# Sums of second-layer weights on GpSimd in 16 tasks, another place for a table of token weights, and another order of one chunk

## The chip, the cores and the metric

The kernel runs on one core of one Trainium2 chip. The metric is the device time of one execution in microseconds (us). The core has five engines that run their own instruction streams in order and wait for each other by semaphores: PE (TensorE, the matmuls), DVE (VectorE), ACT (ScalarE), POOL (GpSimd), and SP, which here issues nearly all DMA transfers. A transfer that waits on SP holds up every transfer behind it on SP.

## The reference

Block-sparse attention over 4 batches of 768 tokens (8 heads of 64), then a mixture of 4 experts on its 3072 x 512 result, weighted by the normalised `domain_probs`:

```python
p = domain_probs / (domain_probs.sum(-1, keepdims=True) + 1e-09)
for e in range(E):
    h = np.maximum(x @ w1[e], 0.0)
    out += p[:, e:e + 1] * (h @ w2[e])
```

Here `x` is 3072 x 512, `w1[e]` 512 x 1024, `w2[e]` 1024 x 512, everything in fp32.

## The kernel before

**Work and stages.** Attention of batch 0 comes first. After that the expert stage of batch b runs interleaved with the attention of batch b + 1. The hidden width of all experts is cut into 8 chunks of 512 (`NCH`). Each fp32 operand of a product is kept as two parts, a rounded one and the rest, and a product of two operands takes three matmuls. ACT writes the rounded part (a cast), POOL or DVE the rest (a subtraction).

**Fewer products.** The chunk products are split into 2 x 2 blocks and done in seven block products instead of eight, which needs sums and differences of blocks of the weights. Chunk 0 of each batch is "plain": eight block pairs, 16 products, in the order of the table `FIRST` (L455). An item (s, half, g) of it is one result, made by two products (k = 0 and 1); s and half name a quarter of the chunk's hidden width, g a half of the tokens. The other chunks follow `ORDER` (L450), with 7 products for each s.

**Weights, once made, are kept.** In batch 0, `operands()` (L494) turns raw first-layer weights `r1` into tiles `wo` (L513 on ACT, L514 on POOL), of which `NWO` = 7 exist, and stores each in DRAM (`kept1`, L492). Later batches load them back in the order of use (L528). Each `next(weights)` makes or loads one more tile; it can go only into a tile whose products are done. `split_w2` (L559) does the same for the second layer as batch 0 uses it (L550 ACT, L551 POOL, store L561).

**Sums of the second layer.** Later batches also need block sums of `w2`. `sums_w2()` (L572) makes them during batch 0, as a generator that is advanced by one `yield` for each step of the expert stage. It has 32 tasks of 8 steps: load 2 x 128 KB (L587), four 128 x 128 subtractions on DVE (L598, L599, L601, L602), a cast of 128 x 512 on ACT (L606), the rest on POOL (L608), four stores of 128 KB (L614). Rows in these transfers are 512 bytes long. Four tiles `r3` rotate.

**Batch 0 on PE.** `first` (L644) makes hidden values in PSUM; ACT (`hh`, L651) and DVE (`hl`, L652) turn each into two parts; DVE also combines block products (`p` L677, `u` L684 and L686, `z` L689). `second` (L695) multiplies with `w2` (L703) into three PSUM tiles `po`, which DVE adds up as `oacc` (L716 for chunk 0, L718). PE can start the next use of a `po` tile only when `oacc` has read it.

**From batch 0 to batch 1.** After the last step of `first`, `experts()` drains what is left of `sums_w2`, closes the pool `raw` (which holds `r1`, `r2`, `r3`), and opens in its memory a pool for `pb`, the token weights spread over partitions; two of them are loaded (L729). From batch 1 on, `first7` (L734) multiplies each hidden block with `pb` (L745, DVE), which releases its PSUM tile, and `second7` (L849) makes the second layer from `ho` and `w2o`, with `w2o` loaded by `again2` (L543). The results of batch 0 go out from `oacc` at L720.

**What sets the order.** Every engine's order is the program's (`manual_schedule`), so the generators' steps fix it:

```python
if c == 0:
    half, k, g = n
    i = [item for item, _ in FIRST].index((s, half, g))
    if k == 0:
        W[0] = ps_m.tile([P, HS], F32, name="vw"[i % 2], bufs=2 - i % 2)
    product(W[0], w, x, k == 0)
    if k == 1:
        finish(half, g, W.pop(0))
        for _ in range(FIRST[i][1]):
            next(weights, None)
```

A weight tile of the plain chunk is used twice, first for g = 0 and last for g = 1, and is free after that.

## Time and profile before

| | |
|---|---|
| time, three executions | 1297.15 us median (1295.63, 1297.15, 1300.03) |
| profiled execution | 1300.79 us, of which the span from first to last instruction is 1298.7 us |
| busy over the span: PE, DVE, ACT, POOL | 1228.8, 901.1, 526.9, 789.0 us |
| granted TensorE clock, mean | 0.984 |
| DMA | 336.25 MB, mean 259 GB/s |

The profile is one execution. A row of the timeline gives the start in us, the duration in us, engine, line, operation and tiles, and in brackets how long the engine sat idle before it and what ended that. A row of the windows gives a stretch's busy us of PE, PEld (weight loading), DVE, ACT and POOL, the granted clock as a share of full speed, the busy share of the DMA engines, and GB/s. Times in all views count from the first instruction. The attention of batch 0 ends at about 104 us, batch 0's experts run to 443 us, batch 1's plain chunk starts there.

### The profile page before, as it was taken

The page shows a single profiled execution, that of the slowest core. Times are in us where ns is not written, and L with a number is a line of the kernel's source. Part 1 is how long each engine was busy: PE and PEld are TensorE (multiplying, and loading weights), DVE is VectorE, ACT ScalarE, POOL GpSimd, SP SyncE. Part 2 cuts the span into 40 slices and gives each one's busy share as a digit, 9 for nine tenths or more (in the row PEclk, how much of TensorE's full clock was granted, in tenths as well). Part 3 has the DMA queues.
Part 4 walks back from the last instruction along what each step waited for, and adds up shares of the span by engine and source line. Part 5 has one row for each costly group of instructions (what it writes and reads, how often), then busy time and mean ns, then how long its engine had stood idle before and what let it go on. Part 6 is the DMA issues. An engine that isn't in the chain of part 4 may idle for free.

```text
span 1298.7 us, 33124 instructions
## 1 busy us (share of the span) xinstructions
PE 1228.8 (95%) x12575; PEld 1121.0 (86%) x12575; DVE 901.1 (69%) x1898; ACT 526.9 (41%) x1261; POOL 789.0 (61%) x702
## 2 busy tenths in 40 slices
PE   6778999999999989999999999999999999999997
PEld 3557778787788778999999989999999999999997
DVE  5455678878787546777766666767776776666667
ACT  3564446554554224444442324444443323222221
POOL 5443547766765255667664665767664777666663
PEclk9889999999999989999999999999999999999999
DMA  8667689999999967889877976989897768888774
GB/s 250 160 197 274 200 279 312 327 318 330 340 329 299 322 203 218 273 266 276 267 247 214 309 224 208 280 260 280 272 258 220 239 221 273 254 261 256 241 242 154
DMA packets 258793, 336.25 MB, mean 259 GB/s; under 512 B 20715, under 2 KB 169804, under 8 KB 258636
## 3 DMA queue, kind: packets, MB, share of 16 engines
q1 hardware_dynamic: 251552, 311.08, 75.7%
q0 software_dynamic: 7040, 23.07, 6.1%
q8 instruction: 99, 1.62, 0.5%
q14 instruction: 58, 0.48, 0.1%
q10 hardware_dynamic: 44, 0.00, 0.0%
HBM read 266.39 MB, written 67.68 MB: 257 GB/s over the span
## 4 chain that ended last, share of the span: by engine, by line
PE 62%; DVE 5%; DMA 3%; issue 1%; SPq 1%; ACT 0%; POOL 0%; DVEq 0%; POOLq 0%; ACTq 0%
PE w L633 16%; PE u L867 15%; PE v L633 12%; PE v L867 11%; PE o L293 2%; PE po L703 2%; PE tp L280 2%; DMA wo<-kept 1%; PE s L258 1%; PE s L253 1%; PE sw L327 1%; DVE ha L745 1%; DVE xo L404 1%; DVE tot L877 1%; PE ow L358 1%
## 5 line engine op out<-in xcount | busy, mean ns | idle before, releaser
L791 POOL TENSOR_TENSOR ho<-ha,ho 128x768 fp32r<-128x768 f32 x165 | 322.1, 1963 | 240.4 <-ACT ho L790 239.8
L633 PE MATMUL w<-xo,wo 128*128 128x384 f32 x1536 | 317.9, 343 | 16.6 <-DMA wo<-kept 6.4
L633 PEld LDWEIGHTS w<-xo,wo 128*128 128x128 f32 x1536 | 272.3, 189 | 30.8 <-DMA wo<-kept 6.1
L790 ACT CAST ho<-ha 128x768 fp32r<-128x768 f32 x168 | 139.4, 836 | 276.7 <-DVE ha L745 92.4
L633 PE MATMUL v<-xo,wo 128*128 128x384 f32 x1200 | 246.0, 341 | 2.7 <-DVE hl L652 2.2
L867 PE MATMUL u<-ho,w2o 128*128 128x384 f32 x1128 | 232.2, 341 | 0.3 <-issue 0.3
L633 PEld LDWEIGHTS v<-xo,wo 128*128 128x128 f32 x1200 | 214.6, 190 | 8.8 <-DVE hl L652 2.8
L867 PEld LDWEIGHTS u<-ho,w2o 128*128 128x128 f32 x1128 | 200.5, 189 | 2.5 <-issue 1.2
L867 PE MATMUL v<-ho,w2o 128*128 128x384 f32 x888 | 182.1, 341 | 1.9 <-issue 1.5
L867 PEld LDWEIGHTS v<-ho,w2o 128*128 128x128 f32 x888 | 156.8, 188 | 3.7 <-issue 2.0
L877 DVE TENSOR_TENSOR tot<-v,tot 128x384 f32<-128x384 f32 x184 | 97.7, 550 | 58.8 <-PE v L867 56.5
L877 DVE TENSOR_TENSOR tot<-u,tot 128x384 f32<-128x384 f32 x180 | 98.9, 552 | 55.3 <-PE u L867 52.6
L703 PE MATMUL po<-w2o,hh 128*128 128x512 f32 x384 | 124.8, 406 | 9.9 <-DVE oacc L718 6.6
L271 ACT ACTIVATE p<-p,mx 128x256 f32<-128x256 f32 (+1 forms) x192 | 95.4, 498 | 82.1 <-DVE mx L268 82.1
L745 DVE SCALAR_TENSOR_TENSOR ha<-ha,pb 128x384 f32<-128x384 f32 x126 | 123.4, 979 | 4.4
L138 POOL DMA_INDIRECT v<-in_vr_dram,vidx x88 | 85.3, 969 | 67.4 <-PE o L293 21.2
L514 POOL TENSOR_TENSOR wo<-r,wo 128x256 fp32r<-128x256 f32 x92 | 75.3, 823 | 74.5 <-ACT wo L513 57.2
L268 DVE CUSTOM_DVE_ANT_1 p<-s,mask 128x256 f32<-128x256 f32 (+1 forms) x192 | 69.7, 417 | 32.1 <-PE s L258 32.0
L703 PEld LDWEIGHTS po<-w2o,hh 128*128 128x128 f32 x384 | 68.3, 188 | 21.6 <-DVE oacc L718 9.8
L703 PE MATMUL po<-w2o,hl 128*128 128x512 f32 x192 | 75.7, 394 | 0.0
L293 PEld LDWEIGHTS o<-v,pt 128*32 128x32 f32 x2816 | 48.6, 116 | 17.7 <-issue 12.8
L293 PE MATMUL o<-v,pt 128*32 128x64 f32 x2816 | 57.4, 229 | 6.8 <-issue 3.5
(149 smaller groups left out, 1659.7 us busy)
## 6 DMA issues: line engine op xcount, KB each, us to landing
w2o<-kept SPq DMA_DIRECT2D x336, 256.0 KB
wo<-kept SPq DMA_DIRECT2D x318, 256.0 KB
kept<-wo SPq DMA_DIRECT2D x106, 256.0 KB
v<-in_vr_dram SPq DMA_DIRECT2D x44, 384.0 KB
kept<-w2o SPq DMA_DIRECT2D x32, 512.0 KB
r<-in_w_dram SPq DMA_DIRECT2D x16, 512.0 KB
r<-in_w_dram SPq DMA_DIRECT2D x32, 256.0 KB
r<-in_w_dram SPq DMA_DIRECT2D x64, 128.0 KB
```

The source lines that it names most:

```text
L138: nc.gpsimd.indirect_dma_start(out=v[:, i, 1], out_offset=None, in_=vr, element_offset=b * S * DM, in_offset=bass.IndirectOffsetOnAxis(ap= ...
L268: nc.vector.tensor_tensor_reduce(p.rearrange("p (a b) -> p a b", b=BLOCK), s[h][:n, i], mk, -SCALE, 3.0e38, ALU.add, ALU.min, mx[:n])
L271: nc.scalar.activation(p, p, AF.Exp, bias=mx[:n], scale=-1.0, accum_out=self.sums[:n, m:m + 1])
L293: nc.tensor.matmul(o[cs, m], self.pt[:, 2 * m + k, cs], vs[c][:, k, e], start=k == 0, stop=k == 1)
L514: nc.gpsimd.tensor_sub(o[:, 1], src, f32(o[:, 0]))
L633: nc.tensor.matmul(ps, w[:, wi, t], x[:, xi, t], start=fresh and m == 0, stop=m == 3 * KH - 1, skip_group_check=not fresh)
L703: nc.tensor.matmul(p, a[:, js], w[:, i], start=f == 0 and n == 0, stop=f == FT - 1 and n == 2)
L745: nc.vector.scalar_tensor_tensor(block(g, half), src, 0.0, q, op0=ALU.max, op1=ALU.mult)
L790: nc.scalar.copy(o[:, 0], src)
L791: eng.tensor_sub(o[:, 1], src, f32(o[:, 0]))
L867: nc.tensor.matmul(ps, w[:, j, wi, ds], h[:, hi, j], start=fresh and m == 0, stop=m == 5, skip_group_check=not fresh)
L877: nc.vector.tensor_add(t, ps, t)
```

## The change

1. `sums_w2` has 16 tasks of 16 steps. A task takes both halves of a pair of rows: one load of 512 KB, four 128 x 256 subtractions on POOL instead of DVE in steps 0 to 3, the two casts (ACT) and rests (POOL) of 128 x 512 in steps 5 and 7, and four stores of 256 KB in steps 8 and 10. Rows in these transfers are 2 KB long. Two tiles `r3` of twice the size rotate. Bytes and the number of steps are the same.
2. `r1` gets a pool of its own, `raw1`, opened before `raw`. The pool of `pb` therefore lies over the two `r1` tiles. Draining `sums_w2`, closing and loading `pb` come three steps of `first` earlier.
3. In later batches the plain chunk follows `FIRST7`: the items (1, 0, 1) and (1, 1, 0) change places, and one weight is loaded after each product with g = 1, where two were loaded after each second one. Batch 0 keeps `FIRST`.

```diff
@@ -49,6 +49,7 @@
     xp = ctx.enter_context(tc.tile_pool(name="xp", bufs=1))
     wp = ctx.enter_context(tc.tile_pool(name="wp", bufs=4, side="right"))
     only_raw = ctx.enter_context(ExitStack())
+    raw1 = only_raw.enter_context(tc.tile_pool(name="raw1", bufs=2, side="right"))
     raw = only_raw.enter_context(tc.tile_pool(name="raw", bufs=2, side="right"))
     dram = ctx.enter_context(tc.tile_pool(name="dram", bufs=1, space=bass.MemoryType.DRAM))
     at = ctx.enter_context(tc.tile_pool(name="at", bufs=2))
@@ -454,6 +455,7 @@
 
     FIRST = [((0, 0, 0), 0), ((0, 1, 0), 0), ((1, 0, 0), 0), ((0, 0, 1), 2), ((0, 1, 1), 2),
              ((1, 1, 0), 0), ((1, 0, 1), 2), ((1, 1, 1), 2)]
+    FIRST7 = [(0, 0, 0), (0, 1, 0), (1, 0, 0), (0, 0, 1), (0, 1, 1), (1, 0, 1), (1, 1, 0), (1, 1, 1)]
     XOF = {(0, 0): 1, (1, 0): 2, (0, 1): 7, (1, 1): 3}
     PLAIN8 = [(s, (i, k)) for s in range(2) for i in range(2) for k in range(2)]
 
@@ -476,7 +478,7 @@
 
     def load_w1(c, s):
         if c < NCH:
-            r1[c, s] = raw.tile([P, 2, 2, KH, P], F32, name="r1")
+            r1[c, s] = raw1.tile([P, 2, 2, KH, P], F32, name="r1")
             nc.sync.dma_start(r1[c, s], w1[c, s])
 
     def load_w2(n):
@@ -571,49 +573,46 @@
 
     def sums_w2():
 
-
-        cols = P
-        tasks = [(c, j, h) for c in range(NCH) for j in range(2) for h in range(2)]
+        half = DM // 2
+        tasks = [(c, j) for c in range(NCH) for j in range(2)]
         r3 = {}
-
-        def part(t, s, h):
-            return t.rearrange("p (d e) -> p d e", d=2)[:, :, h * cols:(h + 1) * cols]
 
         def load(i):
             if i < len(tasks):
-                c, j, h = tasks[i]
-                r3[i] = raw.tile([P, 2, 2, cols], F32, name="r3", bufs=4)
-                for s in range(2):
-                    nc.sync.dma_start(r3[i][:, s], part(w2[c, 2 * s + j], s, h))
+                c, j = tasks[i]
+                r3[i] = raw.tile([P, 2, DM], F32, name="r3", bufs=2)
+                nc.sync.dma_start(r3[i], w2[c, j::2].rearrange("s p e -> p s e"))
 
         load(0)
-        load(1)
         for _ in range(8):
             yield
-        for i, (c, j, h) in enumerate(tasks):
-            load(i + 2)
-            yield
+        for i, (c, j) in enumerate(tasks):
             r = r3.pop(i)
-            b11, b12, b21, b22 = (r[:, s, d] for s in range(2) for d in range(2))
-            nc.vector.tensor_sub(b11, b12, b11)
-            nc.vector.tensor_sub(b12, b22, b12)
-            yield
-            nc.vector.tensor_sub(b22, b22, b11)
-            nc.vector.tensor_sub(b21, b21, b22)
-            yield
-            yield
-            hi = later["t"].tile([P, 2, 2, cols], F32R, name="t2", bufs=2)
-            nc.scalar.copy(hi, r)
-            lo = r.bitcast(F32R)
-            nc.gpsimd.tensor_sub(lo, r, f32(hi))
-            yield
-            yield
-            for s in range(2):
-                k = kept2[c, 1, s, j] if h else keep2(c, 1, s, j)
-                for m, t in enumerate((f32(hi), r)):
-                    nc.sync.dma_start(part(k[:, m], s, h), t[:, s])
-            yield
-            yield
+            b11, b12, b21, b22 = (r[:, s, d * half:(d + 1) * half] for s in range(2) for d in range(2))
+            sums = (b11, b12, b11), (b12, b22, b12), (b22, b22, b11), (b21, b21, b22)
+            parts = {}
+
+            def part(s):
+                hi = later["t"].tile([P, DM], F32R, name="t2", bufs=2)
+                nc.scalar.copy(hi, r[:, s])
+                nc.gpsimd.tensor_sub(r[:, s].bitcast(F32R), r[:, s], f32(hi))
+                parts[s] = f32(hi), r[:, s]
+
+            def store(s):
+                k = keep2(c, 1, s, j)
+                for m, t in enumerate(parts[s]):
+                    nc.sync.dma_start(k[:, m], t)
+
+            for step in range(16):
+                if step < 4:
+                    nc.gpsimd.tensor_sub(*sums[step])
+                if step == 2:
+                    load(i + 1)
+                if step in (5, 7):
+                    part((step - 5) // 2)
+                if step in (8, 10):
+                    store((step - 8) // 2)
+                yield
 
     spare = sums_w2()
 
@@ -746,14 +745,14 @@
 
         if c == 0:
             half, k, g = n
-            i = [item for item, _ in FIRST].index((s, half, g))
+            i = FIRST7.index((s, half, g))
             if k == 0:
                 W[0] = ps_m.tile([P, HS], F32, name="vw"[i % 2], bufs=2 - i % 2)
             product(W[0], w, x, k == 0)
             if k == 1:
                 finish(half, g, W.pop(0))
-                for _ in range(FIRST[i][1]):
-                    next(weights, None)
+            if g:
+                next(weights, None)
             return
         if n in (5, 2, 3):
             v = ps_m.tile([P, HS], F32, name="v", bufs=2)
@@ -917,7 +916,7 @@
                 after_first = True
                 if p > L + 2:
                     next(spare, None)
-                if p == len(one):
+                if p == len(one) - 3:
                     for _ in spare:
                         pass
                     only_raw.close()
@@ -935,7 +934,7 @@
         for b in range(1, B):
             for c in range(NCH):
                 one += ([(b, c, s, n) for s, n in ORDER] if c else
-                        [(b, 0, s, (half, k, g)) for (s, half, g), _ in FIRST for k in range(2)])
+                        [(b, 0, s, (half, k, g)) for s, half, g in FIRST7 for k in range(2)])
                 ends.append(len(one))
                 two += [(b, c, i) for i in range(len(SEQ))]
                 due += [len(one) + 2 + i for i in range(len(SEQ))]
```

How the instructions stand on the engines, at the three places.

**A task of sums, late in batch 0.** DVE before; `r` is the tile `r3`, `hl` the rest of a hidden block, `p` a combined block product, `po` the PSUM tile of the second layer:

```order
L689 TENSOR_TENSOR z_6790<-w,z_6790 128x384
L652 SCALAR_TENSOR_TENSOR hl_6903<-z_6790,hh_6902 128x384
L601 TENSOR_TENSOR r_6631<-r_6631 128x128
L602 TENSOR_TENSOR r_6631<-r_6631 128x128
L652 SCALAR_TENSOR_TENSOR hl_6934<-w,hh_6933 128x384
L598 TENSOR_TENSOR r_6761<-r_6761 128x128
L599 TENSOR_TENSOR r_6761<-r_6761 128x128
L677 TENSOR_TENSOR p_6956<-w,p_6956 128x384
L652 SCALAR_TENSOR_TENSOR hl_7003<-p_6956,hh_7002 128x384
L601 TENSOR_TENSOR r_6761<-r_6761 128x128
L602 TENSOR_TENSOR r_6761<-r_6761 128x128
L718 SCALAR_TENSOR_TENSOR oacc<-po,pr,oacc 128x512 x3
```

DVE now, at the same place:

```order
L688 TENSOR_TENSOR z_6618<-w,z_6618 128x384
L651 SCALAR_TENSOR_TENSOR hl_6728<-z_6618,hh_6727 128x384
L651 SCALAR_TENSOR_TENSOR hl_6757<-w,hh_6756 128x384
L676 TENSOR_TENSOR p_6775<-w,p_6775 128x384
L651 SCALAR_TENSOR_TENSOR hl_6822<-p_6775,hh_6821 128x384
L717 SCALAR_TENSOR_TENSOR oacc<-po,pr,oacc 128x512 x3
```

The sums are gone from between the block products and `oacc`. POOL now, for one task (L608 are the sums, L598 the rests; L516 and L553 are what L514 and L551 were):

```order
L608 TENSOR_TENSOR r_5597<-r_5597 128x256
L516 TENSOR_TENSOR wo<-r_5277,wo 128x256
L608 TENSOR_TENSOR r_5597<-r_5597 128x256 x3
L516 TENSOR_TENSOR wo<-r_5277,wo 128x256
L598 TENSOR_TENSOR r_5597<-r_5597,t_5916 128x512
L516 TENSOR_TENSOR wo<-r_5590,wo 128x256
L598 TENSOR_TENSOR r_5597<-r_5597,t_5936 128x512
```

The four sums now stand in the queue in which POOL also makes the first-layer weights.

**The end of batch 0 on SP.** Before; `kept_0_1_10` is the seventh of the eight weights of batch 1's plain chunk:

```order
L528 DMA wo<-kept_0_0_11_2395 128x512
L528 DMA wo<-kept_0_1_00_2425 128x512
L528 DMA wo<-kept_0_1_01_2583 128x512
L614 DMA kept_7_1_0_1_7041<-t_7090 128x2x128
L614 DMA kept_7_1_0_1_7041<-r_6887 128x2x128
L614 DMA kept_7_1_1_1_7044<-t_7090 128x2x128
L614 DMA kept_7_1_1_1_7044<-r_6887 128x2x128
L528 DMA wo<-kept_0_1_10_2590 128x512
L729 DMA pb<-prt 128x6x128 x2
L720 DMA out_dram<-oacc 128x512 x3
L561 DMA kept_7_0_1_1_7039<-w2o 128x1024
```

Now:

```order
L530 DMA wo<-kept_0_0_11_2398 128x512
L604 DMA kept_7_1_0_1_6877<-t_6848 128x512
L604 DMA kept_7_1_0_1_6877<-r_6629 128x512
L604 DMA kept_7_1_1_1_6880<-t_6864 128x512
L604 DMA kept_7_1_1_1_6880<-r_6629 128x512
L728 DMA pb<-prt 128x6x128 x2
L530 DMA wo<-kept_0_1_00_2428 128x512
L530 DMA wo<-kept_0_1_01_2586 128x512
L530 DMA wo<-kept_0_1_10_2593 128x512
L719 DMA out_dram<-oacc 128x512 x3
```

The last stores of the sums and the two loads of `pb` stand ahead of three weight loads that they stood behind.

**Batch 1's plain chunk on PE, last ten products.** Before; `xo1`, `xo2` belong to g = 0, `xo7`, `xo3` to g = 1, and a `wo` number is a tile of weights:

```order
L633 MATMUL w_7298<-xo7_7170,wo_6962 128x384 x6
L633 MATMUL w_7298<-xo3_7185,wo_7006 128x384 x6
L633 MATMUL v_7317<-xo7_7170,wo_7030 128x384 x6
L633 MATMUL v_7317<-xo3_7185,wo_7059 128x384 x6
L633 MATMUL w_7335<-xo1_7148,wo_7126 128x384 x6
L633 MATMUL w_7335<-xo2_7139,wo_7313 128x384 x6
L633 MATMUL v_7354<-xo7_7170,wo_7079 128x384 x6
L633 MATMUL v_7354<-xo3_7185,wo_7104 128x384 x6
L633 MATMUL w_7373<-xo7_7170,wo_7126 128x384 x6
L633 MATMUL w_7373<-xo3_7185,wo_7313 128x384 x6
```

Now:

```order
L632 MATMUL w_7110<-xo7_6982,wo_6781 128x384 x6
L632 MATMUL w_7110<-xo3_6997,wo_6825 128x384 x6
L632 MATMUL v_7129<-xo7_6982,wo_6846 128x384 x6
L632 MATMUL v_7129<-xo3_6997,wo_6875 128x384 x6
L632 MATMUL w_7147<-xo7_6982,wo_6908 128x384 x6
L632 MATMUL w_7147<-xo3_6997,wo_6928 128x384 x6
L632 MATMUL v_7171<-xo1_6960,wo_6946 128x384 x6
L632 MATMUL v_7171<-xo2_6951,wo_7117 128x384 x6
L632 MATMUL w_7185<-xo7_6982,wo_6946 128x384 x6
L632 MATMUL w_7185<-xo3_6997,wo_7117 128x384 x6
```

The eighth weight (`wo_7313` before, `wo_7117` now) is loaded into the tile that the first of these products frees. It was used as the sixth of these products, and is now used as the eighth.

## The prediction

> **What bounds the kernel now.** I read the page first.
>
> ```profile
> PE 1228.8 (95%) x12575; PEld 1121.0 (86%) x12575; DVE 901.1 (69%) x1898; ACT 526.9 (41%) x1261; POOL 789.0 (61%) x702
> ```
>
> PE is the bound, and the matmuls do not change. Only time in which PE is idle, or runs at a lower clock, can be won. Next I asked what PE waits for, in batch 0's expert stage while the sums run (130 to 440 us) and then at the change of batches (440 to 475 us).
>
> ```profile
> PE po L703 <- DVE oacc L718: 6.6, 5, 2.7
> PE po L703 <- DVE oacc L716: 3.2, 1, 3.2
> PE w L633 <- DVE z L689: 2.1, 5, 0.6
> PE o L293 <- DMA v<-in_vr_dram: 1.7, 2, 1.2
> PE w L633 <- DVE hl L652: 1.4, 2, 1.0
> ```
>
> ```profile
> PE w L633 <- DMA wo<-kept: 5.7, 1, 5.7
> PE w L633 <- DVE ha L745: 1.7, 1, 1.7
> ```
>
> The columns are total us, times, longest. In batch 0 PE waits for DVE: 6.6 + 3.2 + 2.1 + 1.4 = 13.3 us. At the change of batches two waits make 7.4 us. The places, in the timeline of PE, and in that of DVE ahead of the two longest:
>
> ```profile
> 163.86 0.73 PE L703 MATMUL po<-w2o,hh 128*128 128x512 f32 x2 [3.18 <-DVE oacc L716]
> 338.96 0.73 PE L703 MATMUL po<-w2o,hh 128*128 128x512 f32 x2 [2.67 <-DVE oacc L718]
> 154.46 5.30 DVE L598 TENSOR_TENSOR r<-r 128x128 f32<-128x128 f32 x1
> 329.56 5.24 DVE L598 TENSOR_TENSOR r<-r 128x128 f32<-128x128 f32 x1
> 154.99 1.29 POOL L608 TENSOR_TENSOR r<-r,t 128x512 fp32r<-128x512 f32 x1
> 158.18 1.42 POOL L514 TENSOR_TENSOR wo<-r,wo 128x256 fp32r<-128x256 f32 x2
> ```
>
> Each of these two waits follows one sum (L598) that stood on DVE for over 5 us, and in the first case POOL ran instructions one after the other from 154.99 to 159.60, until just before the sum ended at 159.76. Here is what such operations cost over the stage (us busy, mean ns), and one sum undisturbed (minimum, median and maximum in ns):
>
> ```profile
> L598 DVE TENSOR_TENSOR r<-r 128x128 f32<-128x128 f32 x32 | 24.8, 774 | 0.0
> L599 DVE TENSOR_TENSOR r<-r 128x128 f32<-128x128 f32 x32 | 18.7, 584 | 1.1
> L602 DVE TENSOR_TENSOR r<-r 128x128 f32<-128x128 f32 x32 | 14.7, 460 | 1.1
> L601 DVE TENSOR_TENSOR r<-r 128x128 f32<-128x128 f32 x32 | 14.5, 452 | 0.4
> L598 DVE TENSOR_TENSOR r<-r x32: 275/286/5301, 143.9 to 423.2; 128x128 f32<-128x128 f32 x32
> L652 DVE SCALAR_TENSOR_TENSOR hl<-z,hh 128x384 fp32r<-128x384 f32 x14 | 14.9, 1065 | 12.4 <-ACT hh L651 11.8 <-issue 0.6
> L652 DVE SCALAR_TENSOR_TENSOR hl<-w,hh 128x384 fp32r<-128x384 f32 x15 | 8.4, 557 | 8.8 <-ACT hh L651 7.9 <-ACT w2o L550 0.6 <-issue 0.3
> ```
>
> The 128 sums take 72.7 us on DVE, against 128 x 0.286 = 36.6 us at the median of one. The same operation with both inputs in SBUF (`hl<-z`) takes 1065 ns, with one in PSUM (`hl<-w`) 557: I read this so that DVE instructions that read SBUF twice are held up beside POOL, and others are not.
>
> **The sums (part 1).** DVE loses 72.7 us in about 300. POOL gains 64 subtractions of 128 x 256. The nearest rows are the same size on POOL, and the stage by stretches:
>
> ```profile
> L514 POOL TENSOR_TENSOR wo<-r,wo 128x256 fp32r<-128x256 f32 x81 | 66.6, 826 | 62.5 <-ACT wo L513 45.3 <-DMA r<-in_w_dram 7.9 <-issue 4.1
> L514 POOL TENSOR_TENSOR wo<-r,wo x92: 718/744/1452, 81.6 to 416.6; 128x256 fp32r<-128x256 f32 x92
> 160.00:190.00 30.00, 26.82 (x232) 21.18 (x232) 22.49 (x52) 13.43 (x34) 13.62 (x15) 0.94 0.93 300
> 190.00:220.00 30.00, 28.76 (x366) 24.47 (x365) 25.27 (x59) 17.17 (x47) 22.54 (x28) 1.00 0.91 288
> 340.00:370.00 30.00, 30.00 (x385) 26.44 (x382) 23.42 (x63) 15.60 (x44) 17.59 (x23) 0.95 1.01 333
> sum 300.00, PE 285.82 PEld 240.87 DVE 235.88 ACT 155.42 POOL 185.97; mean PE 28.58 PEld 24.09 DVE 23.59 ACT 15.54 POOL 18.60
> ```
>
> At the mean 64 x 0.826 = 53 us; bounds 64 x 0.718 = 46 and 64 x 1.452 = 93 us. POOL goes from 186 of 300 us to about 239 (80%), at most 279; in its fullest stretch, 190 to 220, from 22.5 to 27.8 of 30. PE waits nowhere for POOL in the rows above, and POOL's idle time ends mostly with ACT, so I cost this at nothing: it stands in POOL's gaps, and weights are made up to seven tiles ahead. If that cover is gone, the second rival below is the price.
>
> What PE gets back: the two long waits go, 3.18 + 2.67 = 5.9 us. After each, the stretch shows a lower clock: 0.94 and 0.95 of 30 us, so 0.06 x 30 + 0.05 x 30 = 3.3 us. Together **9.2 us**. What is late next is `hl` and the remaining `oacc` waits, 13.3 - 5.9 = 7.4 us. Some have sums directly in front, others an `hl` that POOL held up. A fuller POOL holds up each remaining one longer: the 42 `hl` of `z`, `p`, `u` lose about 0.5 us each at most now (1065 - 557), and 53/186 = 28% more POOL time adds about 0.14 us each, 6 us of DVE, off PE's path except near an `oacc`. Bounds for this remainder: 7.4 us won, or 3 us lost (each of the 16 groups of three `oacc` later by 0.2 us). I take 1 us lost. Batch 0: **8.2 us** won.
>
> The Trainium skill, page "SBUF — State Buffer", section "Who interferes with whom", speaks against this part: a DVE instruction with two SBUF inputs and a GpSimd instruction that reads SBUF exclude each other, and the second to issue waits for the whole of the first. By it the sums hold the same resource wherever they run, 36.6 us on DVE at the median and 64 x 0.744 = 47.6 us on POOL, and the remaining `hl` would wait more, not less: that is the first rival. The rows above agree with the exclusion (1065 against 557 ns), but the block products and `oacc`, which read PSUM, are held up only by standing behind a sum in DVE's queue, and that goes.
>
> The longer rows of the transfers (2 KB for 512 bytes) and 80 transfers fewer on SP I cost at nothing: the bytes are the same, and PE waits for a transfer in batch 0 for 1.7 us only. Bounds: 1.7 us won, 1.7 lost.
>
> **The change of batches (parts 2 and 3).** SP, DVE and PE there:
>
> ```profile
> 440.26 0.43 SPq L528 DMA_DIRECT2D wo<-kept  x1
> 443.10 0.95 SPq L729 DMA_DIRECT2D pb<-prt  x2
> 444.14 2.05 SPq L720 DMA_DIRECT2D out_dram<-oacc  x3
> 456.00 16.33 SPq L528 DMA_DIRECT2D wo<-kept  x10
> 448.70 0.56 DVE L745 SCALAR_TENSOR_TENSOR ha<-v,pb 128x384 f32<-128x384 f32 x1 [3.55 <-DMA pb<-prt]
> 451.60 2.35 PE L633 MATMUL w<-xo,wo 128*128 128x384 f32 x12 [1.71 <-DVE ha L745]
> 453.80 2.28 PE L633 MATMUL v<-xo,wo 128*128 128x384 f32 x12
> 455.92 1.21 PE L633 MATMUL w<-xo,wo 128*128 128x384 f32 x6
> 462.87 2.29 PE L633 MATMUL w<-xo,wo 128*128 128x384 f32 x6 [5.74 <-DMA wo<-kept]
> 464.95 2.82 PE L633 MATMUL v<-xo,wo 128*128 128x384 f32 x12
> ```
>
> SP stood from 440.7 to 443.1 before `pb`, which lies over tiles of the sums and must wait for their last stores. `pb` landed at 448.7, DVE read it late, and PE waited 1.71 us for the PSUM tile. Behind `pb` came a burst of results and `w2o`, and the eighth weight could be issued only at 456.00. It landed after 6.9 us; PE waited 5.74.
>
> Now `pb` stands three weight loads earlier and waits only for `r1`. Its two loads go out some 10 us earlier, so the 1.71 us go. Two products take 455.92 - 453.80 = 2.12 us. The first product with g = 1 starts at 451.60 - 1.71 = 449.9 and frees the tile at 451.0. The eighth weight is needed at 449.9 + 3 x 2.12 + 1.06 = 457.3. The first three results and most of `w2o` are issued as their inputs get ready, by my estimate from about 436 on, instead of in one row from 444.1 on; SP reaches the eighth weight at about 451. Even with the 6.9 us that it took, it would land at 457.9, 0.6 us late; with less queued ahead of it, in time. The 5.74 us go too, and with them the slow clock after it: six matmuls took 464.95 - 462.87 = 2.08 us for 1.06, and the next twelve 2.82 for 2.28, together 1.6 us. Sum 1.71 + 5.74 + 1.6 = **9.0 us**; bounds 0 (the weight comes later by as much as PE does) and 9.0. I take 8.5. The three steps of draining put two casts and two rests close together on ACT and POOL, which the last step of batch 0 covers.
>
> The new order in batches 2 and 3 removes little: PE waited for `wo<-kept` once more, 0.7 us.
>
> ```profile
> PE w L633 <- DMA wo<-kept: 0.7, 1, 0.7
> ```
>
> One quarter of the hidden values is ready one item (2.1 us) later for `ho`; the last item, which `ho` also waits for, stands where it stood. I take 0.3 us won, bounds 0.7 and -2.
>
> The page "TensorE: Matmul & The Clock Gate", section "What's actually happening", of the Trainium skill says that the clock falls to half after an idle window of about 3.4 us. By that alone waits of 3.18 and 2.67 us would cost no clock and the sum would be 3.3 us smaller; the rows at 0.94 and 0.95 say otherwise, and they decide.
>
> **Sum.** 8.2 + 8.5 + 0.3 = 17.0 us. The profiled execution took 1300.79 us, so 1283.8. The median shown is 1297.15, 3.6 us less than the profiled one. Waits of 5 us on DVE need not come in each execution, so part of what I count as won may already be missing in the median: I subtract half of the 3.6 and predict **1282 us**.
>
> **Rivals.**
> 1. The hold-ups move to what is left on DVE: `hl` instead of L598 stands behind a fuller POOL, and the two long waits of PE stay. For it: `hl<-z` already takes 1065 ns. Against it: only L598 was ever held over 5 us. Then 0 us in batch 0 and 8.8 after it: 1300.8 - 8.8 - 1.8 = 1290.
> 2. POOL's queue becomes the bound, **slower**. A cast waits for sums that stand 4 steps ahead of it; the 264 steps of the sums fill about 300 us, so 4 steps are 4.5 us. Two sums, a weight and a rest of 128 x 512 take 3 x 0.826 + 1.29 = 3.8 us and fit. With the two gathers of one load of `v` they don't:
>
> ```profile
> L138 POOL DMA_INDIRECT v<-in_vr_dram,vidx x22 | 21.5, 977 | 5.1 <-issue 4.2 <-DMA kept<-t 0.3 <-PE o L293 0.2
> ```
>
>    3.8 + 2 x 0.98 = 5.8 us, 1.3 too long. ACT then stands, and behind it the copies that free PSUM for PE. There are 11 such pairs in the stage. If all 1.3 us fall on PE, at each, and the two long waits stay, that is 14 us: 1300.8 - 8.8 + 14 - 1.8 = 1304. It is slower than before from 9 us on, 0.8 us at each pair. Against it: POOL is idle for 114 of the 300 us.
> 3. The eighth weight stays late: only pb's 1.7 us are won at the change of batches, 1282 + 6.8 = 1289.
> 4. Neither place moves: sums and `pb` were late for another reason; 1297.
>
> **How the numbers follow.** Forecast 0.55, rival 1 0.17, rival 3 0.13, rival 4 0.07, rival 2 0.08. About 0.3% (3.9 us) is what a measurement of this kernel can tell from no change, so "faster" is below 1293.3. Rivals 1 and 3 lie 3 and 4 us below that, so a tenth of their 0.30 counts as "same", beside rival 4: faster 0.82, same 0.10, slower 0.08. The range goes down to 1282 - 7.4 - 1 - 1.7 - 0.9 = 1271 (all waits for DVE and transfers in batch 0 go too) and up to 1296, which takes in rivals 1 and 3.
>
> **What would show it.** Right: no wait of PE for `oacc` over 2 us, clock 1.00 from 160 to 370 us, POOL near 80% busy in the stage, `pb` issued before 436 us, no wait for `wo<-kept` in the plain chunk. Wrong: DVE's `hl` over 2 us in many places, ACT's casts of the sums waiting for POOL, SP reaching the eighth weight after 453 us.

## The result, and the profile after

| | median us | runs, lowest to highest | profiled execution | span |
|---|---|---|---|---|
| before | 1298.59 | 1295.63 to 1300.03 | 1300.79 | 1298.7 |
| after | 1283.90 | 1280.73 to 1288.28 | 1286.78 | 1284.6 |

The ratio is 0.989, with an interval of 0.985 to 0.993: faster by 14.7 us. The prediction was 1282 us, range 1271 to 1296. The total is as forecast; the shares of it are not.

The page of the kernel after, busy time by engine:

```profile
PE 1227.5 (96%) x12575; PEld 1122.6 (87%) x12575; DVE 852.3 (66%) x1770; ACT 527.6 (41%) x1261; POOL 836.2 (65%) x766
```

PE does the same work. DVE has lost 49 us and POOL gained 47. The next line is the group of the sums on POOL, 130 to 430 us, in batch 0's expert stage (us busy, mean ns):

```profile
L608 POOL TENSOR_TENSOR r<-r 128x256 f32<-128x256 f32 x64 | 50.9, 795 | 4.3 <-DMA r<-in_w_dram 2.3
```

Forecast: 53 us. What PE waits for in that stage, 130 to 430 us, and (last line) from 440 to 475 us (total, times, longest):

```profile
PE po L702 <- DVE oacc L715: 3.9, 1, 3.9
PE w L632 <- DVE z L688: 2.0, 2, 1.3
PE po L702 <- DVE oacc L717: 1.6, 2, 1.3
...
PE v L632 <- DMA wo<-kept: 3.0, 1, 3.0
```

The waits for DVE fell from 13.3 to 3.9 + 2.0 + 1.6 = 7.5 us. One long wait is still there. At the change of batches, the wait for `ha` has gone, and a shorter wait for the eighth weight remains. The stage by windows (busy us of each engine, granted clock, DMA share, GB/s):

```profile
160.00:190.00 30.00, 26.14 (x221) 19.71 (x221) 19.82 (x32) 10.54 (x28) 18.13 (x22) 0.89 0.87 307
340.00:370.00 30.00, 30.00 (x360) 26.22 (x360) 16.61 (x44) 18.86 (x50) 26.36 (x31) 1.00 1.00 344
130.00:430.00 300.00, 291.51 (x2948) 247.63 (x2941) 193.24 (x398) 159.87 (x418) 236.59 (x285) 0.99 0.91 318
```

POOL is busy for 236.6 of 300 us (79%). The low clock around 340 to 370 us is gone, that after 160 us is not. Why, the timeline says (start us, us, engine, line; in brackets the idle time before and who ended it):

```profile
158.69 1.31 POOL L553 TENSOR_TENSOR w2o<-r,w2o 128x512 fp32r<-128x512 f32 x1
159.94 1.44 POOL L516 TENSOR_TENSOR wo<-r,wo 128x256 fp32r<-128x256 f32 x2
161.32 1.27 POOL L553 TENSOR_TENSOR w2o<-r,w2o 128x512 fp32r<-128x512 f32 x1
162.54 0.72 POOL L516 TENSOR_TENSOR wo<-r,wo 128x256 fp32r<-128x256 f32 x1
163.22 0.71 POOL L608 TENSOR_TENSOR r<-r 128x256 f32<-128x256 f32 x1
159.32 5.04 DVE L651 SCALAR_TENSOR_TENSOR hl<-p,hh 128x384 fp32r<-128x384 f32 x1 [0.59 <-ACT hh L650]
164.28 1.40 DVE L715 TENSOR_SCALAR oacc<-po,pr 128x512 f32<-128x512 f32 x2
165.08 0.79 PE L702 MATMUL po<-w2o,hh 128*128 128x512 f32 x2 [3.86 <-DVE oacc L715]
```

`hl` stood on DVE for 5.04 us. Six POOL instructions ended inside it, and it ended only when POOL paused, after 163.93. Then `oacc`, then PE, 3.86 us late. Before, a sum stood there in the same way; now it is an `hl`.

At the change of batches, SP (start us, us of a group of issues):

```profile
426.33 1.06 SPq L728 DMA_DIRECT2D pb<-prt  x2
428.76 3.82 SPq L530 DMA_DIRECT2D wo<-kept  x3
432.67 1.82 SPq L719 DMA_DIRECT2D out_dram<-oacc  x3
...
436.44 3.92 SPq L545 DMA_DIRECT2D w2o<-kept  x6
440.45 1.49 SPq L719 DMA_DIRECT2D out_dram<-oacc  x2
442.27 1.62 SPq L545 DMA_DIRECT2D w2o<-kept  x2
443.98 0.55 SPq L719 DMA_DIRECT2D out_dram<-oacc  x1
444.62 19.63 SPq L530 DMA_DIRECT2D wo<-kept  x12
```

and PE, from the first product of the plain chunk to the first matmul behind it:

```profile
433.09 2.24 PE L632 MATMUL v<-xo,wo 128*128 128x384 f32 x12
...
449.90 2.29 PE L632 MATMUL v<-xo,wo 128*128 128x384 f32 x6 [2.98 <-DMA wo<-kept]
451.98 3.98 PE L632 MATMUL w<-xo,wo 128*128 128x384 f32 x12
...
457.98 1.49 PE L328 MATMUL sw<-k,qe 64*32 64x384 f32 x16
```

`pb` is issued 17 us earlier than before; 10 us of that is the earlier start of the chunk, ahead of which it now goes out by 6.8 us instead of 0.3. The eighth weight, the first of the twelve `wo` from 444.62 on, goes out 11.5 us after the chunk began (12.6 before). After the wait twelve matmuls took 3.98 us for 2.28.

Where the 14.1 us of span went, by the starts of the same matmuls before and after: 0.35 ahead of batch 0's expert stage (104.27 and 103.92), **9.9** in it (the plain chunk starts at 443.37 and 433.09), **3.65** at the change of batches (28.54 and 24.89 us from there to the first matmul behind), 0.2 in all the rest (826.8 and 826.6).

### The profile page after: what moved, and what is told of

Its sections match the earlier page's. It is cut to its first block, busy times and chain, and to the rows that moved or that the text cites. A ratio compares the mean times of both kernels' runs of the same rounds, so it can differ in the third digit from the quotient of the medians.

```text
span 1284.6 us, 32792 instructions
## 1 busy us (share of the span) xinstructions
PE 1227.5 (96%) x12575; PEld 1122.6 (87%) x12575; DVE 852.3 (66%) x1770; ACT 527.6 (41%) x1261; POOL 836.2 (65%) x766
## 4 chain that ended last, share of the span: by engine, by line
PE 78%; DVE 7%; DMA 5%; issue 4%; POOL 4%; ACT 1%; SPq 1%; DVEq 0%; POOLq 0%; ACTq 0%
PE w L632 18%; PE u L866 15%; PE v L632 14%; PE v L866 11%; PE po L702 6%; PE o L294 3%; PE tp L281 3%; PE sw L328 2%; PE s L259 2%; DMA kept<-wo 2%; PE s L254 2%; DMA wo<-kept 1%; PE ow L359 1%; DVE hl L651 1%; POOL wo L516 1%
## 5 line engine op out<-in xcount | busy, mean ns | idle before, releaser
L516 POOL TENSOR_TENSOR wo<-r,wo 128x256 fp32r<-128x256 f32 x92 | 72.9, 799 | 43.8 <-ACT wo L515 43.6
```

Of the source, the lines that this page charges most:

```text
L516: nc.gpsimd.tensor_sub(o[:, 1], src, f32(o[:, 0]))
```

## The experiments

The kernels ran in three groups, each on one chip beside the kernel before. The median of before was 1289.55, 1299.27 and 1300.64 us there, so only ratios are compared across groups.

| group | kernel | median us | ratio to before, interval |
|---|---|---|---|
| 1 | sums_only | 1275.77 | 0.9892 (0.9862 to 0.9921) |
| 1 | rest_only | 1287.79 | 0.9989 (0.9970 to 1.0007) |
| 1 | pb_only | 1288.03 | 0.9984 (0.9968 to 1.0000) |
| 1 | first7_only | 1288.70 | 0.9984 (0.9965 to 1.0003) |
| 2 | after_again | 1280.56 | 0.9862 (0.9832 to 0.9891) |
| 2 | dve16 | 1289.63 | 0.9929 (0.9904 to 0.9953) |
| 2 | pool32 | 1300.26 | 1.0009 (0.9991 to 1.0027) |
| 2 | no_sums | 1283.74 | 0.9872 (0.9840 to 0.9903) |
| 3 | pool32_loose | 1298.13 | 0.9989 (0.9969 to 1.0008) |
| 3 | tight16 | 1287.34 | 0.9898 (0.9875 to 0.9921) |
| 3 | w2o_late | 1278.92 | 0.9836 (0.9811 to 0.9861) |
| 3 | out_act | 1287.21 | 0.9897 (0.9875 to 0.9918) |

The next table is read from the one profiled execution of each kernel. The stage is batch 0's, from its first matmul `v<-xo,wo` to the first one of the plain chunk; the chunk goes from there to the first matmul behind it. The fifth column is ACT's idle time ahead of the casts `t` of the sums, 130 to 430 us. The last names the DVE instructions of over 4 us in the stage.

| kernel | sums | stage, us | chunk, us | ACT idle ahead of `t`, us | DVE over 4 us |
|---|---|---|---|---|---|
| before | 32 on DVE | 338.8 | 28.5 | 30.1 | two sums |
| rest_only | 32 on DVE | 339.6 | 23.9 | 28.9 | two sums |
| pb_only | 32 on DVE | 339.5 | 27.1 | 28.2 | two sums |
| first7_only | 32 on DVE | 339.4 | 25.3 | 26.0 | two sums |
| sums_only | 16 on POOL | 324.4 | 29.4 | 11.8 | none |
| after | 16 on POOL | 328.8 | 24.9 | 11.8 | one `hl` |
| after_again | 16 on POOL | 324.4 | 24.8 | 11.0 | none |
| w2o_late | 16 on POOL | 324.2 | 19.9 | 11.9 | none |
| out_act | 16 on POOL | 331.1 | 30.6 | 14.2 | one `hl` |
| tight16 | 16 on POOL, casts early | 330.9 | 23.2 | 20.3 | none |
| dve16 | 16 on DVE | 329.3 | 25.0 | 3.4 | one `hl` |
| no_sums | 16, left out | 326.9 | 24.3 | 0.0 | one `hl` |
| pool32 | 32 on POOL | 343.6 | 26.9 | 61.1 | none |
| pool32_loose | 32 on POOL, casts late | 339.1 | 26.1 | 28.7 | none |

**The parts alone.** `sums_only` is the kernel before with the change's `sums_w2` and nothing else:

```
-        tasks = [(c, j, h) for c in range(NCH) for j in range(2) for h in range(2)]
+        tasks = [(c, j) for c in range(NCH) for j in range(2)]
...
+                    nc.gpsimd.tensor_sub(*sums[step])
```

> Part 1 alone (the sums in 16 tasks on GpSimd; one raw pool, loading of pb and the order of the plain chunk as before). Theory: the 10 us by which batch 1's plain chunk starts earlier after the change (433.1 against 443.4 us) come from part 1, so the chunk starts at 432 to 435 us, the two waits after it (1.7 for ha, 5.7 for wo<-kept) stay, and the time is about 10 us below before, ratio 0.992. Rival: part 1 only moves hold-ups from one DVE instruction to another and the gain comes from the other parts: chunk start above 440 us, ratio 0.998 or more.

`rest_only` is the changed kernel with the old `sums_w2`:

```
-                    nc.gpsimd.tensor_sub(*sums[step])
+            nc.vector.tensor_sub(b11, b12, b11)
```

> Parts 2 and 3 alone (sums as before on VectorE in 32 tasks). Theory: nothing changes up to the plain chunk (start at 441 to 445 us); the stretch from there to the first matmul of the next attention scores (28.5 us before, 24.9 after the change) takes 24 to 26 us; ratio 0.997. Rival (the two halves need each other, because the transfers of the sums still fill the queue): the stretch stays above 27 us, ratio 0.999 or more.

`pb_only` is the kernel before with tiles of their own for `r1` and the earlier draining:

```
-            r1[c, s] = raw.tile([P, 2, 2, KH, P], F32, name="r1")
+            r1[c, s] = raw1.tile([P, 2, 2, KH, P], F32, name="r1")
-                if p == len(one):
+                if p == len(one) - 3:
```

> Part 2 alone (r1 in a pool of its own, pb over it, draining three steps earlier). Theory: only the wait for ha (1.7 us) goes; the eighth weight still stands behind the results and w2o and is waited for by 4 to 7 us; ratio 0.998 to 1.000. Rival: pb was what kept the eighth weight back, so both waits go, 9 us, ratio 0.993.

`first7_only` is the kernel before with the new order of later plain chunks:

```
-            i = [item for item, _ in FIRST].index((s, half, g))
+            i = FIRST7.index((s, half, g))
```

> Part 3 alone (order of the plain chunk in later batches). Theory: the wait for ha of 1.7 us stays, the eighth weight is used 2.1 us later and so is waited for 2.1 us less, 3 to 4.5 us instead of 5.7; ratio 0.998 to 0.999. Rival: the weight is also asked for earlier and lands in time, no wait for wo<-kept, ratio 0.995.

The sums alone bring 13.8 us of 1289.55, more than the 10 that were expected; the other two parts, together or apart, 0.9 to 1.8 us, which their intervals do not tell from nothing. The gain of `sums_only` lies in the stage (324.4 us for 338.8); its chunk is no shorter than before. PE's waits from 430 to 480 us, first in `sums_only`:

```profile
PE w L630 <- DMA wo<-kept: 5.8, 1, 5.8
PE w L630 <- DVE ha L742: 1.3, 1, 1.3
```

and in `rest_only`:

```profile
PE v L635 <- DMA wo<-kept: 3.0, 1, 3.0
```

Parts 2 and 3 remove the wait for `ha` and about half of the wait for the eighth weight, whichever way the sums run. `rest_only`'s chunk takes 23.9 us (437.83 to 461.73), 4.6 less than before's in these two profiles, of which its median shows 1.8; where the others went is not known. The wait of 3.0 us is thus not a consequence of the sums on POOL.

**The changed kernel again.** Nothing is edited.

> The changed kernel once more, beside the kernels below on one chip. If the parts add up (part 1 alone 0.9892, parts 2 and 3 alone 0.9989) the ratio is 0.988. If the hold-up of over 5 us on VectorE (hl, at 159 us in the profile of the change, none in that of part 1 alone) is what part 2 and 3 give back by chance, the profile shows it again in some runs and the ratio is 0.989 to 0.990.

The ratio is 0.9862; 0.988, expected if the parts add up, lies in its interval. Six executions lie between 1278.42 and 1286.86. In its profile no wait for `oacc` is longer than 1.28 us; the wait for the eighth weight is there, 3.05 us. The profiles of `sums_only`, `tight16` and `w2o_late` have no long `hl` either; that of `out_act` has one (5.06 us), with a wait of PE of 3.88 us behind it. The long `hl` thus comes in some executions only.

**Which half of part 1?** The change moves the sums to POOL and also makes 16 tasks out of 32, with 2 KB runs. `dve16` keeps the tasks and puts the sums back:

```
-                    nc.gpsimd.tensor_sub(*sums[step])
+                    nc.vector.tensor_sub(*sums[step])
```

> The changed kernel with its four sums of a task on VectorE again (16 tasks, 64 subtractions of 128 x 256, 2 KB runs, parts 2 and 3 kept). Theory: it is the engine that matters: sums stand in VectorE's queue ahead of block products and oacc, VectorE gets 64 x 0.42 us at least back, holds of over 5 us on a sum return with a wait of PE over 2.5 us, and batch 1's plain chunk starts 4 to 9 us later than with the change; ratio 0.993 to 0.996. Rival: the fewer and longer transfers matter: ratio 0.989 as with the change, chunk start within 2 us of it.

In its profile no sum stands on DVE for more than 2.76 us, where over 5 was expected. An `hl` does, for 4.07 us, and PE waits 2.88 us for the `oacc` behind it.

`pool32` keeps the 32 old tasks and moves their sums:

```
-            nc.vector.tensor_sub(b11, b12, b11)
+            nc.gpsimd.tensor_sub(b11, b12, b11)
```

(and so for the other three).

> The changed kernel with the 32 small tasks of before (512-byte runs, 192 transfers of 128 KB), but their four subtractions of 128 x 128 on GpSimd. Theory (the engine matters): no sum on VectorE, so no hold of over 5 us on a sum; 128 subtractions of about 0.4 us cost GpSimd about as much as now; ratio 0.988 to 0.991, chunk start within 3 us of the change. Rival (the transfers matter): chunk start 4 us or more later than with the change, ratio 0.994 or more.

`no_sums` is the changed kernel without the four subtractions of a task; casts, rests, transfers and steps stay.

```
-                if step < 4:
-                    nc.gpsimd.tensor_sub(*sums[step])
```

> The changed kernel without the four subtractions of each task (the loads, casts, rests and stores stay; later batches use sums that were never made). It shows what the sums still cost on GpSimd. Theory: they stand in GpSimd's gaps, PE wins less than 3 us against the change, ratio 0.986 to 0.988. Rival (a fuller GpSimd holds up VectorE's hl and so PE): PE's waits for VectorE from 130 to 430 us (7.5 us with the change) fall below 3 us and the time by over 4 us, ratio 0.985 or less.

With the table's `rest_only` this gives a square: 32 tasks on DVE 0.9989, 32 on POOL 1.0009; 16 on DVE 0.9929, 16 on POOL 0.9862. `pool32` came out as its rival said (0.994 or more). **The engine is worth nothing with the old tasks and 9.1 us (1289.63 - 1280.56) with the new ones. The tasks are worth more than the engine.** On DVE they bring 0.9989 - 0.9929 = 0.006, or 7.8 us; on POOL 19.7 us (1300.26 - 1280.56). And leaving the sums out altogether gains nothing over making them on POOL: 1283.74 against 1280.56, intervals overlapping. On POOL, in this form, they cost nothing that these runs can tell; the intervals leave room for some 4 us.

In `no_sums` DVE still has two long `hl` (4.04 and 3.47 us), the first and what it does to PE in the timeline:

```profile
157.45 4.04 DVE L649 SCALAR_TENSOR_TENSOR hl<-p,hh 128x384 fp32r<-128x384 f32 x1 [0.59 <-ACT hh L648]
...
162.21 1.22 PE L700 MATMUL po<-w2o,hh 128*128 128x512 f32 x2 [2.86 <-DVE oacc L713]
```

No sum runs anywhere in this kernel. Five POOL instructions ended inside this `hl`. So the hold-up does not need the sums on either engine.

In `pool32` the waits moved to ACT. What ACT waits for most from 130 to 430 us (total, times, longest):

```profile
ACT t L608 <- POOL r L604: 59.3, 24, 4.6
```

In the kernel after, the same wait:

```profile
ACT t L597 <- POOL r L608: 11.8, 14, 1.8
```

One such place in the timeline of `pool32`:

```profile
159.96 0.62 ACT L608 CAST t<-r 128x512 fp32r<-128x512 f32 x1 [4.58 <-POOL r L604]
...
161.55 0.78 DVE L654 SCALAR_TENSOR_TENSOR hl<-p,hh 128x384 fp32r<-128x384 f32 x1 [4.04 <-ACT hh L653]
162.26 1.40 DVE L718 TENSOR_SCALAR oacc<-po,pr 128x512 f32<-128x512 f32 x2
163.05 0.73 PE L705 MATMUL po<-w2o,hh 128*128 128x512 f32 x2 [3.05 <-DVE oacc L718]
```

The cast `t` stands in ACT's queue until POOL has made the last sum; `hh` stands behind the cast, `hl` behind `hh`, `oacc` behind `hl`, PE behind `oacc`. This is the prediction's second rival, link by link, in the form of 32 tasks. It also shows why the engine alone wins nothing at this place. Before, `p` stood behind the sums on DVE until 160.65 us, and the cast waited for them too. In `pool32`, whose stage started 0.6 us earlier, `p` starts at 156.95. Its `hh` still comes only 0.8 us earlier, because the cast ahead of it waits for the sums as before. First two lines from before, then one from `pool32`:

```profile
160.77 0.62 ACT L606 CAST t<-r 128x512 fp32r<-128x512 f32 x1 [4.71 <-DVE r L602]
161.81 0.52 ACT L651 ACTIVATE hh<-p 128x384 fp32r<-128x384 f32 x1
161.00 0.52 ACT L653 ACTIVATE hh<-p 128x384 fp32r<-128x384 f32 x1
```

**Is it the distance of the cast?** In `pool32` the cast stands two steps behind the last sum. `pool32_loose` makes it four:

```
             nc.gpsimd.tensor_sub(b21, b21, b22)
             yield
             yield
+            yield
+            yield
             hi = later["t"].tile(...)
```

(The steps between the tasks are taken out to make room.)

> 32 small tasks with sums on GpSimd (512-byte runs), as in the run that took 1.0009 of before, but the cast of a task stands 4 steps behind its last sum instead of 2. Theory: there ScalarE's cast waited 59.3 us in all for GpSimd's sums, with the casts and activations that PE's chain needs queued behind it; the distance in steps is what was missing. ScalarE's wait for GpSimd's sums falls below 20 us, batch 1's plain chunk starts within 4 us of the change's, ratio 0.986 to 0.991. Rival (the small transfers): the distance changes little, ratio 0.996 or more, with PE waiting for transfers or SP behind.

`tight16` is the changed kernel with its two casts earlier:

```
-                if step in (5, 7):
-                    part((step - 5) // 2)
+                if step in (4, 5):
+                    part(step - 4)
```

> The changed kernel with the two casts of a task 1 and 2 steps behind its last sum (steps 4 and 5) instead of in steps 5 and 7. Theory (distance): ScalarE's wait for GpSimd's sums rises from 11.8 us to over 30, PE's waits for VectorE in batch 0 grow by 3 us or more, ratio 0.989 to 0.995. Rival (only the transfers and the number of tasks matter): ratio as with the change, 0.986 to 0.988.

The distance moves ACT's wait for the sums: it fell from 59.3 to 27.4 us in `pool32_loose` and rose from 11.8 to 20.1 in `tight16` (expected were under 20 and over 30). In time, `pool32_loose` stayed at 0.9989. `tight16`, at 0.9898, lies where it was expected if the distance matters, with an interval that overlaps with that of the kernel after; PE's waits for DVE in its stage make 11.7 us, against 7.5 in the kernel after and 5.0 in `after_again`, and its stage takes 330.9 us without a long `hl`. So in the large tasks the distance seems to cost PE some us. On one chip `pool32_loose` and `tight16` lie 10.8 us apart: two steps more do not give the small tasks what the large ones have.

That does not clear the casts. In `pool32_loose` ACT is still idle for 28.7 us ahead of them, as in `rest_only` (28.9). The cast at 160.08 us comes 3.37 us late, and behind it stand `hh`, `hl`, `oacc` and PE's wait of 2.8 us. In the table the stage is longest where ACT idles most ahead of the casts. The two go together; that one causes the other is not shown. What PE waits for in `pool32_loose`, 130 to 430 us:

```profile
PE o L294 <- DMA v<-in_vr_dram: 4.0, 3, 2.8
PE po L705 <- DVE oacc L718: 2.8, 1, 2.8
PE po L705 <- DVE oacc L720: 2.1, 3, 1.2
```

A wait that was 1.7 us before the change has the top place: attention's `v` comes late. The transfers of these 300 us, in the view of DMA, first in `pool32_loose`:

```profile
DMA packets 79752, 91.84 MB, mean 306 GB/s; under 512 B 6331, under 2 KB 53819, under 8 KB 79712
```

then in the kernel after:

```profile
DMA packets 44510, 95.40 MB, mean 318 GB/s; under 512 B 4781, under 2 KB 5356, under 8 KB 44473
```

The 32 tasks make nearly twice the packets for fewer bytes, and the DMA engines are busier with them (share 0.95 against 0.91). They also take 192 issues on SP (64 loads, 128 stores), and the 16 tasks 80. That may be why `v` is late, but `pool32` and `rest_only`, with the same small tasks, wait only 0.9 and 1.3 us for it, and the other waits of that list are not for transfers. The new tasks also take away ACT's idle time ahead of the casts, wherever the sums stand: 28.9 us in `rest_only`, 3.4 in `dve16`. No run had 16 tasks with 512-byte runs, so what of the tasks' 7.8 to 19.7 us belongs to the packets, to SP's issues, to the number of sums and casts or to ACT's waits ahead of the casts **stays open**.

**What holds the eighth weight?** In the kernel after, six loads of `w2o` stand ahead of it on SP from 436.44 on. `w2o_late` asks for batch 1's first `w2o` tiles behind it:

```
         if n >= NCH * FT:
-            next(weights2)
             return
...
+            if b == 1 and k and i > 3:
+                next(weights2)
```

> The changed kernel with the first four w2o tiles of batch 1 (8 transfers, 2 MB) asked for during the second half of batch 1's plain chunk, behind the eighth weight, instead of at the end of batch 0 ahead of it. Theory: the eighth weight waits behind bytes (the DMA engines are busy from 405 to 450 us); the wait for wo<-kept of 3 us and the half clock after it (about 1.5 us) go, ratio 0.003 to 0.004 below the change, 0.982 to 0.984. Rival: w2o then comes too late for second7, a wait of PE for w2o<-kept of 3 us or more takes its place, ratio as with the change.

The weight goes out with the four `wo` of this line of SP's timeline:

```profile
436.97 3.50 SPq L530 DMA_DIRECT2D wo<-kept  x4
440.52 1.25 SPq L545 DMA_DIRECT2D w2o<-kept  x2
```

and on PE the chunk has one wait for a weight left, 0.54 us in its third item:

```profile
428.59 2.29 PE L631 MATMUL v<-xo,wo 128*128 128x384 f32 x12
...
447.38 1.22 PE L631 MATMUL w<-xo,wo 128*128 128x384 f32 x6
448.52 1.49 PE L328 MATMUL sw<-k,qe 64*32 64x384 f32 x16
```

19.93 us from first to last, against 24.89: the wait for the eighth weight and the slow clock behind it are gone, and nothing waits for `w2o` in exchange. Its ratio, 0.9836, is within what was expected and the lowest of all. On its chip it is 0.6% below `tight16` and `out_act`, with no overlap of the intervals, but in the profiles their stages are 7 us longer too, so not all of that is the edit's; the 5 us of the chunk are. Against the kernel after itself, which ran on other chips, the intervals overlap.

`out_act` takes the results of batch 0 off SP instead:

```
-            nc.sync.dma_start(out[tok * P:(tok + 1) * P, :], accs.pop(tok))
+            nc.scalar.dma_start(out[tok * P:(tok + 1) * P, :], accs.pop(tok))
```

> The changed kernel with batch 0's results stored from ScalarE's queue instead of SP's. The bytes and their time stay, the order on SP loses six transfers ahead of the eighth weight. If the weight is late because SP reaches it late (in the change 3.6 us after its tile is free), its wait of 3 us falls below 1 us, ratio 0.983 to 0.985. If it is late because the DMA engines are full, the wait stays at 2 us or more, ratio as with the change, 0.986 to 0.988.

Inconclusive: it made a wait of its own. The profiled execution was the longest of seven (1295.88 us); in its timeline the casts stand behind the stores in ACT's queue:

```profile
435.48 3.54 ACTq L719 DMA_DIRECT2D out_dram<-oacc  x3
439.06 1.56 ACT L402 CAST xo<-xr 128x768 fp32r<-128x768 f32 x2 [14.13 <-DMA pb<-prt]
439.92 0.96 DVE L405 TENSOR_TENSOR xo<-xr,xo 128x768 fp32r<-128x768 f32 x1 [11.14 <-ACT xo L402]
446.92 4.21 PE L632 MATMUL w<-xo,wo 128*128 128x384 f32 x12 [8.71 <-DVE oacc L717]
```

DVE waits 11.14 us for a cast, and PE 8.71 us for DVE. What SP's three stores alone cost cannot be read from it.

## Why the prediction was right, and where not

**The total is right in part by luck: two errors cancel.** Run alone, part 1 brings 13.8 us (forecast 8.2), and parts 2 and 3 bring 1.8 (forecast 8.8). Of the five signs that the prediction named for being right, two came: POOL near 80%, and `pb` before 436 us. Three did not: PE waited 3.86 us for `oacc`, the clock was 0.89 from 160 to 190 us, and PE waited 2.98 us for `wo<-kept`.

- **Batch 0: forecast 8.2 us, measured 9.9 in the profiled execution.** The size fits this execution, which has a long `hl`. In the three without one and with the casts where the change put them, the stage is 14.4 to 14.6 us shorter than before (324.2 to 324.4 against 338.8), so the forecast was too low. Of the two long waits one went, one stayed in the profiled execution, with an `hl` in the place of a sum: the first rival, once. That rival was priced as all or nothing, and it comes by the execution: `after_again` shows no such wait, and `no_sums` shows it without a sum. The waits that the view lists from 104 to 445 us fell by 7.4 us (19.6 to 12.2); 1.7 of these were for attention's `v`, which the prediction held as a bound of the transfers. PE's idle time in the stage fell by 7.2 us in all. The other 2.7 lie in its busy time, 317.4 us instead of 320.1 for the same matmuls, at the same mean clock (0.98); why is not known.
- **Sums on POOL at nothing: right**, by `no_sums`, as far as its interval can tell. POOL took 50.9 us for them (forecast 53), at 79% of the stage (forecast 80%). "Weights are made up to seven tiles ahead" held: PE waits for no weight of POOL's.
- **"The longer rows of the transfers ... and 80 transfers fewer on SP I cost at nothing: the bytes are the same": this step failed.** The bounds were 1.7 us either way. New tasks with the sums left on DVE bring 7.8 us, and without the new tasks the move to POOL brings none (`pool32`, `pool32_loose`). The prediction gave to the engine alone what the engine brings only together with the tasks. It asked only for the waits that the profile put down to a transfer, and priced neither 35,000 more packets in a stage whose DMA share was 0.95, nor SP's issues, nor the 30 us that ACT stood idle ahead of the casts. Which of these the tasks win by is open. (SP's issues fell by 112, from 192 to 80; 80 was a miscount.)
- **Change of batches: forecast 8.5 us, measured 3.65. The second step that failed** is "SP reaches the eighth weight at about 451", 7.6 us after the chunk's start. It was 11.5 us. The results and `w2o` do go out from 433 on, as forecast, but from 436.44 to 444.62 SP still issues eight `w2o` and three results. With the `w2o` behind it the weight went out 8.4 us after the start (436.97 - 428.59). `pb` did what was forecast, and its 1.71 us went. So the third rival came true in part: 2.98 us of waiting, and 1.0 + 1.7 us of slow clock behind it (6 matmuls in 2.08 us for 1.06, 12 in 3.82 for 2.12). Without these 5.7 us the chunk would take 19.2; forecast were 28.54 - 8.5 = 20.0; `w2o_late` has 19.93. The mechanism was right, the order on SP was what was missing.
- **Later batches: forecast 0.3, measured 0.2.** In the other profiles the same stretch takes 822.4 to 828.3 us, so neither figure can be told from nothing.
- **The second rival** (POOL's queue holds ACT) is real: 59.3 us of ACT's time in `pool32`. In the kernel after it stays at 11.8 us, with no wait over 1.8. In `tight16`, with 20.1 us, PE seems to feel it.

The sum was 17.0 us of profiled time; 14.0 were measured (1300.79 to 1286.78). Batch 0 gave 1.7 more than forecast, the change of batches 4.9 less, and attention ahead of them 0.35 that was not forecast. The median lies 2.9 us below the profiled execution, where 1.8 were taken off.

## What to carry to other kernels

When a change does two things at once (another engine, and other sizes of tasks and transfers), run each alone before the gain is given to either: here the engine alone was worth nothing, and the tasks alone less than half of both. A wait for a weight that was fetched too late is read from the issuing queue: list what stands ahead of it from the moment its tile is free, and move behind it whatever is needed later. Taking one suspect instruction away does not remove a hold-up between two engines while other instructions can be held in the same way.

## What the runs showed of the hardware

A DVE instruction with two inputs in SBUF can wait for a whole train of POOL instructions, not for one: 5.04 us over six in the kernel after, 5.22 us for a sum in `rest_only`, 4.04 us over five in `no_sums`. The kernel after has 98 `hl` of `z`, `p` and `u` and sums of first-layer blocks between 104 and 433 us, all with two inputs in SBUF. 46 of them took over 0.1 us more than the shortest of their kind; one POOL instruction ended inside 41 of these, two inside four, and six inside this one. The Trainium skill, page "SBUF — State Buffer", section "Who interferes with whom", has the second to issue wait for the whole of the first; the 41 agree, and the trains go beyond it. What decides between the two was not found.

A wait of 2.98 us was followed by half the clock. The windows of the kernel after, with the granted clock third from the end:

```profile
445.00:450.00 5.00, 2.02 (x12) 1.70 (x11) 0.56 (x1) 0.00 (x0) 3.02 (x2) 0.89 1.06 389
450.00:455.00 5.00, 5.00 (x16) 5.00 (x17) 0.56 (x1) 0.83 (x1) 1.23 (x1) 0.50 0.38 141
```

So the price of this wait was 5.7 us and not 2.98. The length of a wait alone does not set its price. Behind a wait of 3.05 us in `after_again` the clock was 0.66 from 445 to 450 us and 1.00 from there to 455; behind one of 2.32 us in `tight16` it was 0.66 from 450 to 455; and behind one of 2.65 us in `rest_only`, which ended at 333.46, it stayed at 1.00 from 330 to 340.
